# Linear attention feeding a gated MLP: features stationary, plain float32, x divided by token rows, blocks of 512 tokens with 5 and 7 slices

## The chip, the cores and the metric

The kernel runs on one core of a Trainium2 chip. Its time is the device time of one execution in microseconds (us); the median of 3 runs of the kernel before is 1297.62 us (1297.01 to 1298.93).

In the profile the engines are PE (TensorE, matrix multiply), PEld (the weight loads of TensorE, a record for each load), DVE (VectorE), ACT (ScalarE), POOL (GpSimd) and SP (SyncE, which here issues all the DMAs). A matmul has a *stationary* operand, which a weight load puts into the array first, and a *moving* operand, which is streamed past it; "128x65" in a PEld row is a stationary operand of 128 rows and 65 columns, and "128x256" in a PE row is a moving operand of 128 rows and 256 columns.

## The reference

Eight batches, eight heads, 576 tokens, head size D = 64, F = 128 features. `phi` makes 256 features of a token, and the result of the attention is the input x (4608 tokens by 512) of a gated product with 1536 columns:

```python
def phi(x):
    proj = np.einsum('bhsd,df->bhsf', x, w_phi)
    proj = proj - np.max(np.abs(proj), axis=-1, keepdims=True)
    return np.concatenate([np.exp(proj), np.exp(-proj)], axis=-1)
q_p, k_p = phi(q), phi(k)
kv  = np.einsum('bhsf,bhsd->bhfd', k_p, v)
z   = np.sum(k_p, axis=2)
num = np.einsum('bhsf,bhfd->bhsd', q_p, kv)
den = np.einsum('bhsf,bhf->bhs', q_p, z)[..., None] + 1e-06
x   = num / den                        # to (B*S, H*D)
out = ((x @ w_a) * (x @ w_b)) @ w_out
```

All but the three MLP weights is float32. The weights come as float64 and are decoded in the kernel, each into a high and a low float32r part.

## The kernel before

Two number formats are used on TensorE. *Plain* float32 goes in as it is; the trace has two weight loads and two matmul records for each such product. For *float32r* an operand is first split by ACT (a copy, the high part) and DVE (a subtraction, the low part), and a product is then three matmuls, high by high, high by low and low by high, with one record each.

**Attention** works on pairs of heads, 32 in all (8 batches of 4). Of the 576 tokens of a head, 512 are four chunks of 128, and the remaining 64 of two pairs share a "rest" chunk. For a pair:

- `features` projects k: pk (128 tokens by 2 heads by 128 features). The first 9 pairs do it in plain float32; later ones multiply k, stacked as high over low, by `wk2`, which holds the high and low weights side by side (256 moving columns), and ACT and DVE add the two halves. Then DVE takes the maximum and subtracts it, and ACT makes exp(d) and exp(-d).
- `kv_add` accumulates kv transposed: v with a column of ones (65 columns) is stationary, and 256 feature columns move, one matmul for each chunk and head in the first 11 pairs (plain), three in the later ones.
- `k_finish` copies it out, turns it with four transposes and, after pair 7, splits it.
- `q_side` projects q (plain in the first 2 pairs), has POOL take the maximum over partitions, makes the features, splits them and multiplies: kv is stationary (65 columns), 288 tokens move. Numerators go to `xun` and denominators to `den` in DRAM. `reciprocals` makes 1/(den + eps) of a batch by way of DRAM.

**The MLP** runs in two passes over the 12 slices of 128 of the 1536 columns. The first pass, 6 slices in 16 blocks of 288 tokens, fills the time between the attention's instructions and stores its sum in `part`; the second, 6 slices in 9 blocks of 512, comes after the attention and adds `part`. `load_x` loads x and the broadcast reciprocals, multiplies them and splits the product. A block (`moe_block`) then has, for each slice, 12 matmuls into pa and 12 into pb (L515), the product h, its split (L136, L143), and at the end 4 groups of matmuls into po (L538).

**Order.** `attention_steps` gives each piece of a pair a turn number; after each turn up to `PACE` steps of other work (weight decoding, MLP blocks) are emitted. A scheduler then orders the instructions of each engine with a model of their times, and every engine runs its own list in order. Buffers are named by tag with a number of copies; an instruction that writes a new tile waits until the last reader of the old one is done. Of PSUM the MLP has 3 tiles in the attention's time, the attention 4, and kv 1 (in the first batch one of the MLP's).

Of the kernel before, what the change touches and what calls it, by code (L numbers as in the profile page):

```python
# [19 lines left out]
P = 128  # L20
# [3 lines left out]
TURNS0, TURNS, PAIRS0 = 5, 4, 7  # L24
LOAD_TURNS = (-5, -2, -1)
K_TURNS, K_STEP = (0, 3, 5), 2
REST_LOAD_TURNS = (-5, -1, 0)
# [13 lines left out]
ENGINES = {  # L41
    "k_hi": "vss",
    "k_lo": "vvv",
    "v_hi": "sss",
    "v_lo": "vvv",
    "ke_hi": "sss",
    "q_hi": "vss",
    "q_sub": "vvv",
    "qe_hi": "vss",
}  # L50

SLICES0 = 6
T2 = 512
# [3 lines left out]
def tile_kernel(ctx, tc, qT, km, kr, vm, vr, w_phi, w_a, w_b, w_out, out):  # L57
# [20 lines left out]
    X_CHUNKS = 2  # L78
    TS = (HALF, T2)
    NFS = (SLICES0, DF // P - SLICES0)  # L80

# [16 lines left out]

    def products(a, b):

        if len(a) == 1:
            return [(a[0], b[0])]
        return [(a[0], b[0]), (a[0], b[1]), (a[1], b[0])]

    def attention_consts(a1):
# [12 lines left out]
        wk2 = a1.tile([P, 2, F], F32R, name="wk2")  # L118
        nc.vector.memset(wk2.bitcast(F32), 0.0)
        nc.vector.tensor_copy(wk2[:, 0, :], wh)  # L120
        nc.vector.tensor_copy(wk2[:D, 1, :], wl[:D])
        ident = a1.tile([P, P], F32, name="ident")
        make_identity(nc, ident)
        vaug = []
        for i in range(2):
            t = a1.tile([P, NFULL, 2, D + 1], F32R, name=f"vaug{i}")
            nc.vector.memset(t[:, :, :, D : D + 1].bitcast(F32), 1.0)
            vaug.append(t)
        return w2, wh, wl, wk32, wk2, ident, vaug

    def engine(step, b):
        return {"v": nc.vector, "s": nc.scalar}[ENGINES[step][min(b, 2)]]

    def copy(eng, dst, src):
        if eng is nc.scalar:
            eng.copy(dst, src)  # L136
        else:
            eng.tensor_copy(dst, src)

    def split(hi, lo, src, eng_hi, eng_lo):  # L140

        copy(eng_hi, hi, src)
        eng_lo.tensor_tensor(lo, src, hi, op=ALU.subtract)  # L143

    def stack(hi_lo, src, eng_hi, eng_lo):

        copy(eng_hi, hi_lo, src)
        eng_lo.tensor_tensor(hi_lo[D:], src[D:], hi_lo[D:], op=ALU.subtract)  # L148

    def k_load(b, pr, a1, a2, ps, consts, st):  # L150
        vaug = consts[-1]
# [3 lines left out]
        if i < PLAIN_K:  # L155
            k32 = a1.tile([P, n], F32, tag="ks", bufs=2, name=f"k32_{u}")
            nc.sync.dma_start(k32, km[b, pr])
# [4 lines left out]
        if i < PLAIN_KV:  # L162
            v32 = a1.tile([P, NFULL, 2, D + 1], F32, tag="vl", bufs=2, name=f"v32_{u}")
            nc.vector.memset(v32[:, :, :, D : D + 1], 1.0)
        else:
            v32 = a1.tile([P, NFULL, 2, D], F32, tag="v32", name=f"v32_{u}")
        nc.sync.dma_start(v32[:, :, :, :D], vm[b, pr])
        yield
        st["k", b, pr] = (k32,)
        if i >= PLAIN_K:  # L170
            ks = a1.tile([P, 2, n], F32R, tag="ks", bufs=2, name=f"ks_{u}")
# [123 lines left out]
    def spare(b, ps):  # L295

        return (ps_moe, "moe", 3) if b == 0 else (ps, "kvacc", 1)
# [338 lines left out]
```

## Time and profile before

| | |
|---|---|
| median of 3 runs | 1297.62 us |
| the profiled execution, its own time | 1299.35 us |
| its span, first to last instruction | 1297.6 us |
| PE busy | 1253.2 us, 97% |
| PEld busy | 1114.9 us, 86% |
| DVE busy | 841.9 us, 65% |
| ACT busy | 703.1 us, 54% |
| POOL busy | 157.1 us, 12% |
| moved by DMA | 140.12 MB, mean 108 GB/s |

The program has three stages: to about 95 us attention and weight decoding alone, then attention and first pass mixed to 697 us, and after that the rest of the first pass and the second, which run to the end. A busy time of PE is made of records whose ends are modelled, and which overlap; the distance from one record's start to the next is what a matmul costs where PE has no wait.

### The profile page before, as it was taken

The numbers are of one execution on the slowest core, as the hardware profiler recorded it, in microseconds if no ns is written. First come the engines' busy times: TensorE is split into PE (matmuls) and PEld (weight loads), VectorE is DVE, ScalarE is ACT, GpSimd is POOL, SyncE is SP. The second block draws the span as 40 slices with busy tenths as digits, with TensorE's granted clock in tenths as the row PEclk, the third lists the DMA queues.
The fourth block names the chain that finished last, engine by engine and source line by source line (L and its number), as shares of the span: only waits on it lengthen the run. The fifth ranks groups of instructions, "written<-read, shape, count | busy, mean of one in ns | idle before, by whom it ended". The sixth has DMA issues, their size and how long they took to land.

```text
span 1297.6 us, 20263 instructions
## 1 busy us (share of the span) xinstructions
PE 1253.2 (97%) x7632; PEld 1114.9 (86%) x7632; DVE 841.9 (65%) x1388; ACT 703.1 (54%) x1471; POOL 157.1 (12%) x70
## 2 busy tenths in 40 slices
PE   7989879999999999999999999999999999999998
PEld 4558659999999999999999899988888888888887
DVE  5999985798998989988973532698323323333322
ACT  5777775788989888988884322443211211211210
POOL 2323211131222222221220000000000000000000
PEclk9999979999999999999999999999999999999999
DMA  8666532443433435344224821243233133133100
GB/s 197 169 179 177 155 100 77 110 114 107 132 102 112 134 82 156 87 123 123 55 80 117 241 83 56 66 155 110 73 114 98 49 114 98 49 114 96 51 33 33
DMA packets 116594, 140.12 MB, mean 108 GB/s; under 512 B 29136, under 2 KB 81872, under 8 KB 116496
## 3 DMA queue, kind: packets, MB, share of 16 engines
q1 hardware_dynamic: 116496, 138.83, 37.4%
q8 instruction: 60, 0.98, 0.3%
q14 instruction: 38, 0.31, 0.1%
HBM read 110.18 MB, written 28.61 MB: 107 GB/s over the span
## 4 chain that ended last, share of the span: by engine, by line
PE 53%; DVE 7%; ACT 2%; issue 2%; DMA 2%; SPq 0%; DVEq 0%; ACTq 0%
PE po L538 17%; PE pb L515 16%; PE pa L515 16%; PE kvps L286 2%; PE pn L364 2%; DVE qs L148 1%; DVE kel L143 1%; DMA rb<-rec 1%; DVE qel L143 0%; DVE kd L231 0%; DVE kd L234 0%; DVE ks L148 0%; PE pq L340 0%; DMA den<-xn 0%; DVE x L492 0%
## 5 line engine op out<-in xcount | busy, mean ns | idle before, releaser
L344 POOL PARTITION_ALL_REDUCE mb<-p x64 | 156.4, 2444 | 512.8 <-ACT p L341 304.0
L515 PE MATMUL pa<-xh,wh_a 128*128 128x288 f32 (+1 forms) x600 | 200.2, 334 | 5.3 <-DVE h L520 3.1
L538 PE MATMUL po<-hh,wl_o 128*128 128x288 f32 (+1 forms) x600 | 195.8, 331 | 7.2 <-DVE wl_o L433 7.0
L515 PE MATMUL pb<-xh,wh_b 128*128 128x288 f32 (+1 forms) x600 | 198.8, 331 | 4.1 <-ACT h L519 4.1
L520 DVE TENSOR_TENSOR h<-pb,h 128x288 f32<-128x288 f32 (+1 forms) x150 | 80.5, 538 | 185.9 <-PE pb L515 185.2
L515 PE MATMUL pa<-xl,wh_a 128*128 128x288 f32 (+1 forms) x600 | 198.8, 331 | 0.0
L538 PE MATMUL po<-hl,wh_o 128*128 128x288 f32 (+1 forms) x600 | 198.2, 332 | 0.1
L515 PE MATMUL pb<-xl,wh_b 128*128 128x288 f32 (+1 forms) x600 | 198.0, 330 | 0.0
L515 PE MATMUL pa<-xh,wl_a 128*128 128x288 f32 (+1 forms) x600 | 197.8, 330 | 0.0
L515 PE MATMUL pb<-xh,wl_b 128*128 128x288 f32 (+1 forms) x600 | 197.4, 329 | 0.0
L538 PE MATMUL po<-hh,wh_o 128*128 128x288 f32 (+1 forms) x600 | 196.2, 333 | 1.0 <-ACT o L541 0.5
L136 ACT CAST hh<-h 128x288 fp32r<-128x288 f32 (+1 forms) x150 | 75.3, 502 | 192.5 <-DVE h L520 189.8
L519 ACT COPY h<-pa 128x288 f32<-128x288 f32 (+1 forms) x150 | 70.2, 469 | 186.3 <-PE pa L515 184.5
L538 PEld LDWEIGHTS po<-hh,wl_o 128*128 128x128 f32 x600 | 113.2, 189 | 16.6 <-DVE wl_o L433 7.3
L515 PEld LDWEIGHTS pa<-xh,wh_a 128*128 128x128 f32 x600 | 113.3, 189 | 15.8 <-DVE h L520 4.2
L515 PEld LDWEIGHTS pb<-xh,wh_b 128*128 128x128 f32 x600 | 112.9, 188 | 14.7 <-ACT h L519 5.9
L538 PEld LDWEIGHTS po<-hh,wh_o 128*128 128x128 f32 x600 | 112.8, 190 | 11.1 <-DVE h L520 0.9
L538 PEld LDWEIGHTS po<-hl,wh_o 128*128 128x128 f32 x600 | 113.9, 190 | 9.0 <-DVE hl L143 0.4
L515 PEld LDWEIGHTS pa<-xh,wl_a 128*128 128x128 f32 x600 | 113.6, 189 | 8.6
L515 PEld LDWEIGHTS pa<-xl,wh_a 128*128 128x128 f32 x600 | 113.4, 189 | 8.8 <-issue 0.2
L515 PEld LDWEIGHTS pb<-xl,wh_b 128*128 128x128 f32 x600 | 113.0, 188 | 8.5 <-issue 0.2
L515 PEld LDWEIGHTS pb<-xh,wl_b 128*128 128x128 f32 x600 | 112.9, 188 | 8.5
(131 smaller groups left out, 2339.2 us busy)
## 6 DMA issues: line engine op xcount, KB each, us to landing
q<-in_qT SPq DMA_DIRECT2D x124, 144.0 KB
k<-in_km SPq DMA_DIRECT2D x55, 256.0 KB
xun<-xn SPq DMA_DIRECT2D x64, 144.0 KB
x<-xun SPq DMA_DIRECT2D x32, 288.0 KB
rb<-rec SPq DMA_DIRECT2D x64, 144.0 KB
part<-o SPq DMA_DIRECT2D x16, 576.0 KB
o<-part SPq DMA_DIRECT2D x9, 1024.0 KB
v<-in_vm SPq DMA_DIRECT2D x32, 256.0 KB
```

Of the source, the lines that this page charges most:

```text
L136: eng.copy(dst, src)
L143: eng_lo.tensor_tensor(lo, src, hi, op=ALU.subtract)
L148: eng_lo.tensor_tensor(hi_lo[D:], src[D:], hi_lo[D:], op=ALU.subtract)
L286: nc.tensor.matmul(st["kv_ps", b, pr][:width, j], v_[:, j, :width], e_[:, j], start=(left == NFULL and j == 0 and n_ == 0), stop=(left == ...
L344: nc.gpsimd.partition_all_reduce(mb, p32, P, bass_isa.ReduceOp.absmax)
L364: nc.tensor.matmul(pn[: D + 1, :HALF], kv_[:, 2 * j + s, :], e_[:, s, tok], **at)
L515: nc.tensor.matmul(acc, w[:, cc * P : (cc + 1) * P], x, start=(k == 0), stop=(k == 3 * NCC - 1))
L519: nc.scalar.copy(h32, pab["a"])
L520: nc.vector.tensor_tensor(h32, pab["b"], h32, op=ALU.mult)
L538: nc.tensor.matmul(acc, w[:, cc * P : (cc + 1) * P], h, start=(k == 0), stop=(k == 3 * NFS[p] - 1))
```

## The change

- kv is accumulated with the **features stationary** (128 tokens by 128 features) and v with its column of ones moving (65 columns), in plain float32 in all pairs; for each chunk and head two matmuls, one for each sign. The result is already the way round that the numerators want it: no transposes, no split, one ACT copy.
- The **numerators** also have the features stationary (128 features by 128 tokens of q) and kv moving (65 columns), plain float32 in all pairs; a head's 576 tokens are five tiles, the first and the second overlapping by 64. Tokens now lie on partitions, so x is divided at once by its own denominator (`tensor_scalar_add`, `reciprocal`, multiply); `reciprocals`, `den` and `rec` are gone.
- A new step, `x_finish`, turns a pair's x with five transposes on TensorE, splits it into float32r parts, and stores both in DRAM. `load_x` loads the two parts straight into the matmuls' tiles, one copy of each.
- k's float32r projection has 128 moving columns: for each chunk and head two matmuls into the same sum, with the high and with the low weights. `wk2` and the ACT and DVE addition are gone. Plain float32 now in 6 pairs for k and 4 for q.
- Both passes use **blocks of 512 tokens**, the first with 5 slices, the second with 7; the second starts with the two slices whose weights have places of their own. Turns and paces differ a little, and a batch's blocks are queued 2 turns after it is ready.

```diff
-TURNS0, TURNS, PAIRS0 = 5, 4, 7
+TURNS0, TURNS, PAIRS0 = 5, 4, 5
+X_TURN = 13
-DECODE_TURN, BLOCK_LAG = 2, 8
-PACE0, PACE, PACE0_UNTIL = 0.65, 0.9, 18
-PLAIN_K, PLAIN_Q, PLAIN_KV, PLAIN_NUM = 9, 2, 11, 7
-SLICES0 = 6
-T2 = 512
+DECODE_TURN, BLOCK_LAG = 2, 2
+PACE0, PACE, PACE0_UNTIL = 0.65, 0.8, 18
+PLAIN_K, PLAIN_Q = 6, 4
+SLICES0 = 5
+T = 512
...
+    Q_TILES = [slice(0, P)] + [slice(REST + i * P, REST + (i + 1) * P) for i in range(NFULL)]
+    X_CUTS = (0, REST + NFULL // 2 * P, S)
-    xun = [dpool.tile([DM, S], F32, name=f"xun{b}") for b in range(B)]
-    den = [dpool.tile([H, S], F32, name=f"den{b}") for b in range(B)]
-    rec = [dpool.tile([H, S], F32, name=f"rec{b}") for b in range(B)]
+    xparts = [[dpool.tile([DM, S], F32, name=f"x{n}d{b}") for n in "hl"] for b in range(B)]
...
     def features(u, i, k_, c0, n, a2, ps, consts):
-                for j in range(2):
-                    nc.tensor.matmul(pk[:, j], k_[:, j, (c0 + c) * P : (c0 + c + 1) * P], wk2, start=True, stop=True)
-                nc.scalar.copy(kb[:, to], pk[:, :, 1])
-                nc.vector.tensor_tensor(d[:, to], pk[:, :, 0], kb[:, to], op=ALU.add)
+            for j in range(2):
+                nc.tensor.matmul(pk[:, c, j], k_[:, j, tok], wh, start=True, stop=False)
+                nc.tensor.matmul(pk[:, c, j], k_[:, j, tok], wl, start=False, stop=True)
...
-    def kv_add(b, pr, vs, es, st):
-        for j in range(2):
-            parts = products(vs, es)
-            for n_, (v_, e_) in enumerate(parts):
-                nc.tensor.matmul(
-                    st["kv_ps", b, pr][:width, j],
-                    v_[:, j, :width],
-                    e_[:, j],
+    def kv_add(b, pr, v_, e_, st):
+        for j, s in itertools.product(range(2), range(2)):
+            nc.tensor.matmul(
+                st["kv_ps", b, pr][:, j, s, : D + 1],
+                e_[:, j, s],
+                v_[:, j],
...
     def k_finish(b, pr, a1, a2, ps, consts, st):
-        nc.scalar.copy(kvT[: D + 1], st["kv_ps", b, pr][: D + 1].rearrange("p j (s f) -> p (j s) f", s=2))
-        for g in range(4):
-            nc.tensor.transpose(pt[:, g, : D + 1], kvT[: D + 1, g, :], ident[: D + 1, : D + 1])
+        kv = a2.tile([P, 2, 2, D + 1], F32, tag="kv", name=f"kv_{b}_{pr}")
+        nc.scalar.copy(kv, st["kv_ps", b, pr][..., : D + 1])
...
     def q_side(b, pr, j, a1, a2, ps, consts, st):
-            for n_, (s, kv_, e_) in enumerate(parts):
-                at = dict(start=(n_ == 0), stop=(n_ == len(parts) - 1))
-                nc.tensor.matmul(pn[: D + 1, :HALF], kv_[:, 2 * j + s, :], e_[:, s, tok], **at)
-            nc.scalar.copy(xn[: D + 1, tok], pn[: D + 1, :HALF])
-        nc.sync.dma_start(xun[b][h * D : (h + 1) * D], xn[:D])
-        nc.sync.dma_start(den[b][h : h + 1], xn[D : D + 1])
+        pn = ps.tile([P, n, D + 1], F32, tag="att", name=f"pn_{u}")
+        for t, tok in enumerate(Q_TILES):
+            for s in range(2):
+                nc.tensor.matmul(pn[:, t], e[:, s, tok], st["kv", b, pr][:, j, s], start=(s == 0), stop=(s == 1))
+        nc.vector.tensor_scalar_add(r, pn[:, :, D], EPS)
+        nc.vector.reciprocal(r, r)
+        nc.vector.tensor_tensor(x, pn[:, :, :D], r.unsqueeze(2).broadcast_to([P, n, D]), op=ALU.mult)
+
+    def x_finish(b, pr, a1, a2, ps, consts, st):
+        xh, xl = (a2.tile([P, S], F32R, tag=f"x{n}t", bufs=1, name=f"x{n}t_{b}_{pr}") for n in "hl")
+        for lo, hi in zip(X_CUTS, X_CUTS[1:]):
+            pt = ps.tile([P, 512], F32, tag="att", name=f"pt_{b}_{pr}_{lo}")
+            for t, tok in enumerate(Q_TILES):
+                tok = slice(tok.start, REST if t == 0 else tok.stop)
+                if lo <= tok.start < hi:
+                    n = tok.stop - tok.start
+                    nc.tensor.transpose(pt[:, tok.start - lo : tok.stop - lo], x[:n, t], ident[:n, :n])
+            split(xh[:, lo:hi], xl[:, lo:hi], pt[:, : hi - lo])
+        for to, x_ in zip(xparts[b], (xh, xl)):
+            nc.sync.dma_start(to[pr * P : (pr + 1) * P], x_.bitcast(F32))
...
+    def load_x(p, j):
+        xs = [xpool.tile([P, NCC, T], F32R, tag=f"x{n}", name=f"x{n}_{p}_{j}") for n in "hl"]
+            for src, x_ in zip(xparts[b], xs):
+                to = x_[:, :, t - j * T : t - j * T + n]
+                nc.sync.dma_start(to.bitcast(F32), src.rearrange("(c p) s -> p c s", p=P)[:, :, s0 : s0 + n])
...
+    order = [*range(NFS[0], NFS[1]), *range(NFS[0])]
```

More of the change, by code (lines that the diff above doesn't have):

```diff
@@ L117, in attention_consts, with stack, split @@
             nc.vector.tensor_copy(wk32[rows, j, :], w2[rows, :])
[L118 to L121, printed above, removed]
         ident = a1.tile([P, P], F32, name="ident")
         make_identity(nc, ident)
[L124 to L148, printed above, removed]
+        ones = []
+        for name, n, shape in (("va", 3, [P, NFULL, 2, D + 1]), ("rv", 2, [P, 2, D + 1])):
+            ones.append([a1.tile(shape, F32, name=f"{name}{i}") for i in range(n)])
+            for t in ones[-1]:
+                nc.vector.memset(t[..., D : D + 1], 1.0)
+        return w2, wh, wl, wk32, ident, *ones
+    def stack(hi_lo, src):
+        nc.scalar.copy(hi_lo, src)
+        nc.vector.tensor_tensor(hi_lo[D:], src[D:], hi_lo[D:], op=ALU.subtract)
+    def split(hi, lo, src):
+        nc.scalar.copy(hi, src)
+        nc.vector.tensor_tensor(lo, src, hi, op=ALU.subtract)
     def k_load(b, pr, a1, a2, ps, consts, st):
-        vaug = consts[-1]
         u = f"{b}_{pr}"
@@ L242, in features @@
         nc.scalar.activation(e[:, :, 0, :], d, AF.Exp)
         nc.scalar.activation(e[:, :, 1, :], d, AF.Exp, scale=-1.0)
-        es = (e,)
-        if not plain:
-            eh = a2.tile(shape, F32R, tag=f"keh{n}", bufs=n, name=f"keh_{u}")
-            el = a2.tile(shape, F32R, tag=f"kel{n}", bufs=n, name=f"kel_{u}")
-            split(eh, el, e, engine("ke_hi", i // NPAIR), nc.vector)
-            es = (eh, el)
-        yield es
+        yield e
     def k_chunks(b, pr, c0, a1, a2, ps, consts, st):
@@ L534, in moe_block @@
             k = 0
-            for f, (hh, hl) in enumerate(hs):
+            for f, (hh, hl) in hs.items():
                 hi, lo = weights[(p, f, "o")]
@@ L556, in run @@
                 steps -= 1
-    weights, pools_moe, xpools = {}, [ps_moe], [xpool]
-    per = S // TS[0]
+    weights, pools_moe, late = {}, [ps_moe], []
+    blocks = [moe_block(0, j, range(NFS[0])) for j in range(NT // T)]
     with ExitStack() as c:
@@ L589, in tile_kernel @@
     next(last)
-    for f in range(NFS[1]):
+    for f in order:
         if f < NFS[0]:
             next(last)
-        for _ in load_weights(1, f, "ab", wpool if f < NFS[0] else late, stage):
+        for _ in load_weights(1, f, "ab", wpool if f < NFS[0] else late[0], stage):
             pass
     run(deque([last]))
-    first = moe_block(1, 0)
+    first = moe_block(1, 0, order)
     next(first)
-    for f in range(NFS[1]):
+    for f in order:
         next(first)
-        for _ in load_weights(1, f, "o", wpool if f < NFS[0] else late, stage):
+        for _ in load_weights(1, f, "o", wpool if f < NFS[0] else late[0], stage):
             pass
-    run(deque([first] + [moe_block(1, j) for j in range(1, NT // TS[1])]))
+    run(deque([first] + [moe_block(1, j, order) for j in range(1, NT // T)]))
 def kernel(q, k, v, w_phi, moe_w_a, moe_w_b, moe_w_out):
```

255 lines of the change are left out of this document (81 added, 174 removed).

## The prediction

> **What bounds the kernel now.** I read the page first, then busy times by stage, then TensorE's groups kept apart by shape.
>
> ```profile
> span 1297.6 us, 20263 instructions
> PE 1253.2 (97%) x7632; PEld 1114.9 (86%) x7632; DVE 841.9 (65%) x1388; ACT 703.1 (54%) x1471; POOL 157.1 (12%) x70
> ```
>
> By stage (PE, PEld, DVE, ACT, POOL busy; granted clock; DMA):
>
> ```profile
> 0.00:50.00 50.00, 40.15 (x169) 25.55 (x170) 35.71 (x72) 29.49 (x63) 14.61 (x12) 1.00 0.75 188
> 50.00:100.00 50.00, 43.34 (x191) 26.62 (x189) 47.19 (x77) 37.96 (x84) 17.05 (x8) 0.97 0.66 180
> 100.00:150.00 50.00, 48.54 (x297) 39.89 (x296) 47.15 (x85) 37.85 (x83) 10.35 (x4) 1.00 0.59 159
> 150.00:200.00 50.00, 37.34 (x198) 31.76 (x197) 40.90 (x67) 33.73 (x71) 10.43 (x4) 0.83 0.42 118
> 300.00:697.00 397.00, 391.80 (x2990) 381.21 (x2989) 347.15 (x539) 337.44 (x725) 85.56 (x35) 1.00 0.38 103
> 697.00:760.00 63.00, 59.91 (x433) 58.97 (x432) 27.15 (x60) 19.39 (x47) 0.00 (x0) 0.97 0.67 193
> 760.00:1280.00 520.00, 520.00 (x2583) 446.36 (x2582) 212.08 (x358) 129.83 (x236) 0.00 (x0) 1.00 0.26 82
> ```
>
> From 760 us on PE never stops; from 300 to 697 us it stops for 5 us in 397, although DVE and ACT are 85 to 87% busy too. Only in the first 200 us is there idle time to win, 30.6 us of it. So the change is worth what it does to the sum of TensorE's intervals, plus some part of those early waits.
>
> **The price of a matmul now.** Busy times of PE overlap, so I take the distance between starts. The first two rows are pieces of the chain of waits (start, us, what, count), the others the timeline's, where a merged row's count divides the time to the next row.
>
> ```profile
> 757.14 9.58 PE po L538 x72
> 1277.54 16.33 PE po L538 x72
> ```
>
> ```profile
> 22.78 1.89 PE L286 MATMUL kvps<-ke,v 128*65 128x256 f32 x8
> 24.51 1.86 PE L364 MATMUL pn<-qe,kvh 128*65 128x288 f32 x7
> ...
> 321.77 0.28 PE L286 MATMUL kvps<-keh,vaug 128*65 128x256 f32 x1
> ...
> 323.19 0.30 PE L340 MATMUL pq<-qs,wh 128*128 128x288 f32 x1
> ```
>
> A float32r matmul costs 9.58/72 = 133 ns at 288 columns, 16.33/72 = 226.7 at 512, and (323.19 - 321.77)/12 = 118 at 256 (12 kv matmuls stand between). A plain record of 256 columns costs (24.51 - 22.78)/8 = 216, by width 243 at 288; a plain product has two.
>
> Counts, by shape:
>
> ```profile
> L515 PE MATMUL pa<-xh,wh_a 128*128 128x288 f32 x384 | 116.2, 303 | 5.3 <-DVE h L520 3.1 <-ACT xh L136 1.7 <-ACT o L541 0.4
> L515 PE MATMUL pb<-xh,wh_b 128*128 128x512 f32 x216 | 84.1, 389 | 0.0
> L286 PE MATMUL kvps<-keh,vl 128*64 128x256 f32 x168 | 46.9, 279 | 0.0
> L364 PE MATMUL pn<-qel,kvh 128*65 128x288 f32 x200 | 43.8, 301 | 0.2 <-DVE qel L143 0.2
> L286 PE MATMUL kvps<-ke,v 128*65 128x256 f32 x176 | 43.1, 388 | 0.0
> L228 PE MATMUL pk<-wk,ks 128*128 128x256 f32 x184 | 34.3, 286 | 0.0
> L340 PE MATMUL pq<-qs,wl 128*128 128x288 f32 x120 | 34.2, 296 | 0.0
> L364 PE MATMUL pn<-qe,kvh 128*65 128x288 f32 x112 | 31.2, 415 | 5.5 <-DVE kd L234 3.0 <-ACT kvh L311 1.6 <-DVE kd_r L234 0.7
> L219 PE MATMUL pk<-wk,k 128*128 128x256 f32 x72 | 20.5, 412 | 5.3 <-DMA k<-in_km 5.3
> L286 PE MATMUL kvps<-ke_r,rv 64*65 64x256 f32 x48 | 13.1, 390 | 0.0
> L286 PE MATMUL kvps<-keh_r,rvh 64*65 64x256 f32 x40 | 12.1, 303 | 0.0
> ```
>
> Nine MLP forms of 384 and of 216: 3456 x 133 ns + 1944 x 226.7 = 459.6 + 440.7 = 900.3 us. kv: 3 products x (168 + 40 in the rest chunks) x 118 ns + (176 + 48) x 216 = 73.6 + 48.4 = 122.0. Numerators: 600 x 133 ns + 112 x 243 = 107.0. Transposes: 128 x 62 ns (from the weight loads below) = 7.9. k: (184 + 22) x 118 ns + (72 + 10) x 216 = 42.0 (the rest chunks' 22 and 10 are 11 and 5 groups by two). q: 240 x 133 ns (wl as many as wh) + 16 x 243 = 35.8 (2 pairs, 2 heads, 2 halves, 2 records). Attention 314.7, **all 1215.0 us**; the span is 1297.6, so 82.6 us are waits, start and end. The last piece of po ends at 1293.9, 3.7 us before the end, and the first matmul waited 5.3 us for k: 9 us are not to be had.
>
> **The price of the new form.** kv and the numerators now load 128 feature columns for only 65 moving ones. The trace has no such matmul, but it has the load. These are groups of weight loads, then loads and matmuls around one spot where the queue had run dry:
>
> ```profile
> L228 PEld LDWEIGHTS pk<-wk,ks 128*128 128x128 f32 x184 | 28.0, 191 | 0.5 <-ACT p L341 0.2 <-issue 0.2
> L286 PEld LDWEIGHTS kvps<-kel,vaug 128*65 128x65 f32 x168 | 22.8, 135 | 0.0
> L308 PEld LDWEIGHTS pt<-ident,kvT 65*128 65x128 f32 x128 | 12.5, 144 | 3.4 <-ACT kvT L304 1.6 <-issue 1.4
> ```
>
> ```profile
> 22.47 0.33 PEld L308 LDWEIGHTS pt<-ident,kvT 65*128 65x128 f32 x4 [1.37 <-issue]
> ```
>
> ```profile
> 58.27 0.19 PEld L340 LDWEIGHTS pq<-qs,wh 128*128 128x128 f32 x1 [0.39 <-ACT p L341]
> 58.37 0.19 PEld L340 LDWEIGHTS pq<-qs,wl 128*128 128x128 f32 x1
> ...
> 58.27 0.40 PE L340 MATMUL pq<-qs,wh 128*128 128x288 f32 x1
> 58.51 0.29 PE L340 MATMUL pq<-qs,wl 128*128 128x288 f32 x1
> ```
>
> A load of 63 more columns takes 191 - 135 = 56 ns more, 0.89 ns a column: about 110 ns for 128, the rest latency. The spot says the same: the second load starts 0.10 us after the first, and the second matmul 0.24 after it, which is one load (0.107) and one 288-column matmul (0.133) in a row. So a matmul waits for its own load, the next load starts when the array has taken the one before, and a load of 128 columns is hidden today only because a matmul of 256 or 288 columns lasts longer. Transposes load faster: (0.33 - 0.144)/3 = 62 ns for 128 columns. In a plain record 65 columns stream for 216 x 65/256 = 55 ns. So the new record costs its load, 108 ns, and some 6 ns of handing over: **114 ns**, 228 for a product. Bounds: 62 ns (the transposes' pace) and 108 + 55 = 163 (nothing overlaps). I take 114, since the row's shape is that of an ordinary load, and loads do overlap matmuls in every dense row.
>
> k's float32r matmuls of 128 columns load 128 as well: 114 ns each, for a stream that would last about 59. No row has float32r below 256 columns; the bound above is the plain price, 2 x 216 x 128/256 = 216 ns, the bound below again 62.
>
> **The sum after.**
>
> - MLP: (5 x 24 + 4 x 15) x 9 + (7 x 24 + 4 x 21) x 9 = 1620 + 2268 matmuls x 226.7 ns = 881.4 us (19 less: 512 columns carry the fixed part better than 288).
> - kv: 32 pairs x 5 chunks x 4 products x 2 records = 1280 x 114 ns = 145.9 (24 more).
> - Numerators: 64 heads x 5 tiles x 2 signs x 2 records = 1280 x 114 = 145.9 (39 more).
> - Transposes: 160 x 62 = 9.9 (2 more).
> - k: 26 pairs x 4.5 chunks x 4 = 468 x 114 = 53.4, and 27 plain chunks x 2 x 216 = 11.7: 65.1 (23 more).
> - q: 224 x 133 + 32 x 243 = 37.6 (2 more).
>
> All 1285.8 us, **70.8 more than before**.
>
> What is taken from DVE and ACT lies beside PE, so it pays only through the waits:
>
> ```profile
> L143 DVE TENSOR_TENSOR qel<-qe,qeh 128x1152 fp32r<-128x1152 f32 x50 | 68.7, 1374 | 20.5 <-ACT qeh L136 18.4 <-PE pq L340 2.1
> L143 DVE TENSOR_TENSOR kel<-ke,keh 128x1024 fp32r<-128x1024 f32 x42 | 52.8, 1258 | 0.6 <-ACT keh L136 0.4
> L231 DVE TENSOR_TENSOR kd<-pk,kb 128x256 f32<-128x256 f32 x92 | 35.2, 415 | 0.8 <-ACT ke_r L243 0.4
> ```
>
> These three alone are 157 us of DVE, mostly in the attention's time; the new division and `x_finish`'s splits do for each element once what `load_x` does today in both passes, so they add nothing. DVE was 94% busy between 50 and 150 us, and there PE waited; less of that now, and fewer weights to decode early (15 for 18). But in the first pairs (plain today too) DVE loses little. I take 47 us for waits, start and end instead of 82.6; the ends are 25 (9 and a little) and 83 (nothing won).
>
> The x transfers cost nothing as long as they have the po part of a block: 60 or 84 matmuls, 13.6 or 19.0 us, for 2 MB into single tiles, which can start only after the last pb. Today's order, on SP, and the rates there (1.25 us a figure, from 983 us):
>
> ```profile
> 983.83 0.87 SPq L485 DMA_DIRECT2D x<-xun  x2
> ...
> 1001.01 0.59 SPq L548 DMA_DIRECT2D out_x<-o  x1
> ```
>
> ```profile
> GB/s 0 74 340 13 0 10 172 174 358 132 7 0 0 90 202 258 408 293 7 93 380 360 5 0 0 0 0 0 0 0 0 13 0 0 0 0 0 0 0 0
> ```
>
> The load goes out as po begins, ahead of the store; at 340 to 408 GB/s 2 MB take 5 to 6 us.
>
> So 1285.8 + 47 = 1332.8 us of span. The profiled execution lies 1.75 us over its span (1299.35 to 1297.6), and the median 1.73 below the profiled execution: the two cancel, and I forecast a median of **1333 us**, 2.7% slower.
>
> **Rivals.**
>
> 1. *Faster: loads at the transposes' pace.* If plain feature columns load in 62 ns, all 1280 + 1280 + 468 = 3028 records save 52 ns, 157 us: 1176 us. For it: these transposes do load float32 at that pace. Against: theirs last 144 ns, while the ordinary 128-column loads last 191. The point of decision: 36 us over 3028 records, 12 ns; a record must cost under 102 ns for the kernel not to be slower. The Trainium skill ("TensorE: Matmul & The Clock Gate", Back-to-back issue gap) gives about 81 ns a matmul for a sustained stream of loads and matmuls at N = 128; by it the three forms would be 100 us cheaper than at 114, some 1233 us. The same sentence gives 131 ns for N = 512, where this trace has 226.7, so I hold little of it for 4-byte operands.
> 2. *Narrow float32r at the plain price.* k's 468 matmuls at 216 instead of 114 ns: 48 us more, 1381 us. For it: the kernel before went out of its way to make 256 columns, by `wk2`. Against: no row shows a dependence on width but the streaming itself.
> 3. *x comes late.* If SP puts the load behind the store, or the one copy of x is freed late, each of 17 blocks waits some 6 us: 102 us, 1435. Against: the order above.
> 4. *The early waits vanish altogether* and loads need no handing over: 3028 x 6 = 18 us and 20 us of waits less, 1295: no change.
>
> **Chances.** Forecast 0.66 (own range 1302 to 1369, the two ends of the waits, loads at 108 to 114); rival 1 0.14; rival 2 0.13; rival 3 0.03; rival 4 0.04. The range 1300 to 1390 holds the forecast and rival 2 and leaves out 1 and 3. A measurement of this kernel tells about 0.2% from no change; faster by more 0.14, within 0.04, slower 0.82.
>
> **What would show it.** In the timeline a kv chunk pair of 16 records should take 1.8 us (rival 1: 1.0) with the next record's load starting as each matmul starts; the numerators' 20 records 2.3 us; four narrow k matmuls 0.46 us (rival 2: 0.86). pa's twelve matmuls should stay at 2.72 us in the last stage, which should be 514 us long, 73 longer than 1944 matmuls are now, while the stages before it lose little or nothing. Idle PE between 0 and 200 us should fall below 30 us. I am wrong if TensorE's intervals sum to less than 1250 us, or if waits take more than 83.

## The result, and the profile after

The changed kernel takes 1388.78 us (median of 4 runs, 1378.36 to 1395.91) where the kernel before takes 1298.28 beside it: a ratio of 1.0687 (95% interval 1.0603 to 1.0772). It is 6.9% slower; the forecast was 2.7%. The direction was right, and the size was missed by 56 us. The spread is new as well: the kernel before stays within 5 us, the changed one moves by 17, and by 26 with the four runs of a later repetition (experiment 4). A ratio here leaves out runs that took over 1.5% longer than the fastest of their kernel, which changes a figure in one place: the second run of experiment 6, where the ratio rests on two of its four times and the median on all.

The page of the changed kernel, its totals and the granted clock in 40 equal slices of the span, in tenths:

```profile
span 1376.6 us, 18489 instructions
PE 1347.7 (98%) x7386; PEld 1162.8 (84%) x7386; DVE 616.6 (45%) x1053; ACT 493.5 (36%) x932; POOL 142.8 (10%) x70
...
PEclk9678999999998999999999999999999999999999
```

DVE and ACT are much relieved (45 and 36% busy, from 65 and 54), and PE is 98% busy. Over the whole span PE is idle for 28.9 us (1376.6 - 1347.7), where the kernel before had 44.4 (1297.6 - 1253.2). Taken alone, that reads like a denser TensorE kernel. But the second to fourth slices of PEclk say 6, 7 and 8.

The changed kernel by stage (from and to, length, then PE, PEld, DVE, ACT and POOL busy with counts, granted clock, DMA share, GB/s):

```profile
0.00:50.00 50.00, 41.52 (x222) 34.14 (x223) 34.30 (x70) 24.48 (x49) 12.17 (x11) 0.88 0.66 168
50.00:100.00 50.00, 47.55 (x246) 42.52 (x246) 47.30 (x83) 28.90 (x58) 11.96 (x5) 0.70 0.57 163
100.00:150.00 50.00, 44.91 (x259) 38.98 (x258) 33.46 (x60) 25.06 (x51) 6.92 (x3) 0.87 0.50 140
150.00:200.00 50.00, 50.00 (x325) 44.97 (x325) 24.61 (x42) 23.92 (x46) 8.56 (x4) 1.00 0.39 109
...
770.00:860.00 90.00, 84.59 (x367) 70.00 (x368) 58.64 (x108) 34.34 (x59) 0.00 (x0) 0.96 0.55 184
```

Idle PE in the first 200 us is 16.0 us (8.5 + 2.4 + 5.1 + 0), where it was 30.6 before; 5.3 of the 16.0 are the start's wait for k, as before, and 4.9 are new waits for x. Between 770 and 860 us, where the two passes meet, it is 5.4 us. Yet from 50 to 100 us the clock was 0.70 on average, so for some 30 of these 50 us PE ran at half its clock, and that time counts as busy. The clock in smaller stretches:

```profile
37.00:61.00 24.00, 21.49 (x79) 18.33 (x80) 20.68 (x40) 13.38 (x27) 4.56 (x2) 0.51 0.40 127
61.00:82.00 21.00, 18.69 (x130) 16.19 (x128) 20.25 (x37) 12.97 (x26) 5.13 (x2) 0.99 0.73 208
82.00:103.00 21.00, 20.86 (x89) 18.79 (x87) 19.34 (x34) 11.34 (x24) 4.51 (x2) 0.51 0.55 154
```

There are only two values, half and full. At half clock PE does some 80 to 90 records in 21 to 24 us and looks as busy as at full clock, where it does 130 in 21 us.

The prices, from the changed kernel's timeline (start, us, engine, line, matmul, shapes, count); the distance to the next row divided by the count is the price of one record. The first two rows lie in a stretch of half clock, the others at full clock:

```profile
41.69 4.53 PE L268 MATMUL pn<-kv,qe 128*128 128x65 f32 x20
46.01 2.02 PE L169 MATMUL pk<-wk,k 128*128 128x256 f32 x4
...
297.85 2.34 PE L268 MATMUL pn<-kv,qe 128*128 128x65 f32 x20
300.00 0.31 PE L172 MATMUL pk<-wh,ks 128*128 128x128 f32 x1
300.93 2.62 PE L216 MATMUL kvps<-va,ke 128*128 128x65 f32 x22
303.47 0.86 PE L289 MATMUL pt<-ident,x 64*128 64x64 f32 x5
304.17 2.34 PE L268 MATMUL pn<-kv,qe 128*128 128x65 f32 x20
```

At full clock: numerators (300.00 - 297.85)/20 = 108 ns, eight narrow float32r matmuls (300.93 - 300.00)/8 = 116, kv (303.47 - 300.93)/22 = 115, transposes (304.17 - 303.47)/5 = 140. At half clock a numerator record takes (46.01 - 41.69)/20 = 216 ns: the load doubles like the rest.

With the medians of such distances over the whole trace, the intervals sum to kv 139.5, numerators 139.1, transposes 20.3, k 68.4, q 39.5 and MLP 881.2: 1288.2 us, where 1285.8 was forecast. The span is 1376.6, so 88.4 us are waits, start, end and slow stretches, where 47 were forecast. Such a sum is known to about 1%: with medians over single records, instead of rows of the timeline, it is 1295.6 us (1221.0 for the kernel before), which leaves 81.0 us beside it (76.6 before).

The waits of PE before and after, in two fences (line, what for, us in total, times, longest). The kernel before:

```profile
PE po L538 <- DVE wl_o L433: 7.0, 2, 4.8
...
PE pq L340 <- DVE qs L148: 4.2, 4, 2.2
PE pb L515 <- ACT h L519: 4.1, 6, 1.1
PE pa L515 <- DVE h L520: 3.1, 4, 1.8
PE pn L364 <- DVE kd L234: 3.0, 2, 1.7
```

The changed kernel:

```profile
PE pa L413 <- issue: 7.1, 1, 7.1
...
PE pa L413 <- DMA xh<-xhd: 4.8, 4, 3.3
PE pq L252 <- DVE kd L178: 2.6, 2, 2.3
PE pq L252 <- issue: 2.5, 1, 2.5
PE pa L413 <- DMA xl<-xld: 1.9, 2, 1.6
```

Before, the list is led by DVE and ACT, which have 34 us in the whole of it. After, they are left with 3.3 us, 2.6 of them in the row above, and the first matmul of an MLP block waits for x instead: 4.8 and 1.9 us by name. The 7.1 us "issue" are x too, by the timeline of all engines there:

```profile
767.42 0.86 PE L289 MATMUL pt<-ident,x 64*128 64x64 f32 x5
768.10 0.70 ACT L116 CAST xht<-pt 128x320 fp32r<-128x320 f32 x2
768.83 0.32 SPq L292 DMA_DIRECT2D xhd<-xht  x1
769.41 0.97 SPq L292 DMA_DIRECT2D xld<-xlt  x1
773.07 0.37 SPq L394 DMA_DIRECT2D xh<-xhd  x1
...
775.41 0.76 PE L413 MATMUL pa<-xh,wh_a 128*128 128x512 f32 x1 [7.13 <-issue]
```

The last pair's x is turned, split, stored to DRAM, loaded back and then multiplied; SP issues the load 3.7 us after the store, and PE starts 7.1 us after its last transpose's end.

In summary, the sum of intervals came out nearly as forecast. Two things that the forecast did not contain stand where the old waits were: a clock that is halved for some 55 of the first 140 us, and x that comes late. The runs now separate them.

### The profile page after: what moved, and what is told of

Read it like the earlier page. It is cut to its first block, busy times and chain, and to the rows that moved or that the text cites. A ratio compares the mean times of both kernels' runs of the same rounds, so it can differ in the third digit from the quotient of the medians.

```text
span 1376.6 us, 18489 instructions
## 1 busy us (share of the span) xinstructions
PE 1347.7 (98%) x7386; PEld 1162.8 (84%) x7386; DVE 616.6 (45%) x1053; ACT 493.5 (36%) x932; POOL 142.8 (10%) x70
## 4 chain that ended last, share of the span: by engine, by line
PE 91%; DMA 4%; DVE 3%; issue 1%; ACT 1%; POOL 0%; SPq 0%; ACTq 0%
PE pa L413 22%; PE po L437 22%; PE pb L413 21%; PE pn L268 9%; PE kvps L216 9%; PE pq L252 3%; PE pt L289 2%; PE pk L173 2%; PE pk L172 1%; DMA xl<-xld 1%; DMA xh<-xhd 1%; PE pk L169 1%; DMA xld<-xlt 1%; DMA xhd<-xht 0%; DVE p L257 0%
## 5 line engine op out<-in xcount | busy, mean ns | idle before, releaser
L413 PE MATMUL pa<-xh,wh_a 128*128 128x512 f32 x432 | 172.4, 399 | 11.9 <-issue 7.1
L413 PE MATMUL pa<-xl,wh_a 128*128 128x512 f32 x432 | 171.0, 396 | 1.9 <-DMA xl<-xld 1.9
L413 PE MATMUL pa<-xh,wl_a 128*128 128x512 f32 x432 | 170.0, 394 | 0.0
L437 PE MATMUL po<-hh,wh_o 128*128 128x512 f32 x432 | 169.7, 394 | 0.0
L413 PE MATMUL pb<-xh,wh_b 128*128 128x512 f32 x432 | 169.0, 391 | 0.0
L437 PE MATMUL po<-hl,wh_o 128*128 128x512 f32 x432 | 168.8, 391 | 0.0
L437 PE MATMUL po<-hh,wl_o 128*128 128x512 f32 x432 | 168.6, 390 | 0.0
L413 PE MATMUL pb<-xh,wl_b 128*128 128x512 f32 x432 | 168.3, 390 | 0.0
L413 PE MATMUL pb<-xl,wh_b 128*128 128x512 f32 x432 | 168.2, 389 | 0.0
L268 PE MATMUL pn<-kv,qe 128*128 128x65 f32 x1280 | 161.5, 284 | 0.2
L413 PEld LDWEIGHTS pa<-xh,wh_a 128*128 128x128 f32 x432 | 82.6, 191 | 29.3 <-issue 7.8
```

The source lines that it names most:

```text
L268: nc.tensor.matmul(pn[:, t], e[:, s, tok], st["kv", b, pr][:, j, s], start=(s == 0), stop=(s == 1))
L413: nc.tensor.matmul(acc, w, x[:, cc], start=(k == 0), stop=(k == 3 * NCC - 1))
L437: nc.tensor.matmul(acc, w[:, cc * P : (cc + 1) * P], h, start=(k == 0), stop=(k == 3 * NFS[p] - 1))
```

## The experiments

In what follows, *halved time* is twice the missing share of the granted clock times the span: 77 us in the profiled run of the changed kernel, (1 - 0.972) x 2 x 1376.6, and 23 to 29 in most runs of the kernel before. All edits are to the changed kernel, unless "before" is said.

**1. Wider moving operands.** If a record costs its load, moving columns are free up to about 128. In kv 128 columns of v now move, in the numerators 102; the products that nobody needs are computed and not read.

```diff
-                st["kv_ps", b, pr][:, j, s, : D + 1],
+                st["kv_ps", b, pr][:, j, s],
                 e_[:, j, s],
-                v_[:, j],
+                v_.rearrange("p j d -> p (j d)")[:, 2 * j : 2 * j + P],
...
-        kv = a2.tile([P, 2, 2, D + 1], F32, ...)
-        nc.scalar.copy(kv, st["kv_ps", b, pr][..., : D + 1])
+        kv = a2.tile([P, 2, 2, P], F32, ...)
+        nc.scalar.copy(kv, st["kv_ps", b, pr])
...
+        wide = 512 // n
+        at, to = (0, 0) if j == 0 else (P - wide, wide - D - 1)
-                nc.tensor.matmul(pn[:, t], e[:, s, tok], st["kv", b, pr][:, j, s], ...)
+                nc.tensor.matmul(pn[:, t], e[:, s, tok], st["kv", b, pr][:, j, s, at : at + wide], ...)
```

> The changed kernel with the same weight loads and the same count of records, but wider moving operands in the two new forms: kv moves 128 columns instead of 65 (63 of them the other head's, not used), the numerators 102 instead of 65. Three theories. Load: a record costs the load of its 128 stationary columns, so both forms stay at 112 ns although the array streams 2.0 and 1.6 times as much; were streaming the price, kv would go to some 213 ns and the kernel would be over 130 us slower. Clock: the changed kernel had its TensorE clock halved for 77 us of its profiled run (23.9, 20.5, 10.2, 13.7 and 6.8 us at a time, where the kernel before had 3.4 at a time), because the array streams only 55 of 112 ns; with the wider stream the halved time falls below 25 us in all and the kernel is 25 to 45 us faster than the changed one's 1388.8, between 1345 and 1365. Waits: the clock only follows the waits of the schedule, the width has no part in it, and the time stays between 1378 and 1396.

Measured: 1356.88 us (1355.34 to 1359.09), ratio 1.0444 (1.042 to 1.0467). A kernel that streams more columns in every attention matmul is 32 us faster. The timeline of this kernel, read as above:

```profile
280.02 2.37 PE L270 MATMUL pn<-kv,qe 128*128 128x102 f32 x20
282.17 0.31 PE L172 MATMUL pk<-wh,ks 128*128 128x128 f32 x1
...
283.10 2.67 PE L216 MATMUL kvps<-va,ke 128*128 128x128 f32 x22
285.70 0.86 PE L291 MATMUL pt<-ident,x 64*128 64x64 f32 x5
```

A numerator record takes 2.15/20 = 108 ns, as with 65 columns, and a kv record 2.60/22 = 118, 3 ns more. So a record's price doesn't follow its stream, as the forecast had it, and the gain comes from elsewhere. The clock of the same stretches says where:

```profile
37.00:61.00 24.00, 21.07 (x126) 17.83 (x127) 21.59 (x41) 14.95 (x32) 5.43 (x3) 0.86 0.48 145
82.00:103.00 21.00, 20.22 (x158) 18.72 (x158) 20.19 (x36) 17.45 (x35) 7.07 (x3) 1.00 0.80 236
```

The clock is 0.86 and 1.00 instead of 0.51, and PE does 126 and 158 records where it did 79 and 89. Halved time is 16 to 24 us in the four runs, and the spread of their times has shrunk to 4 us.

**2. Half a load.** In kv only 64 of the 128 features are loaded. This leaves out the other half of the features; their place in kv takes a copy of the first half's sums.

```diff
-                st["kv_ps", b, pr][:, j, s, : D + 1],
-                e_[:, j, s],
+                st["kv_ps", b, pr][:REST, j, s, : D + 1],
+                e_[:, j, s, :REST],
...
```

> The changed kernel with 64 instead of 128 stationary columns in kv's 1280 records: half of the features are left out of kv (the second half of the features takes the first half's sums), all else is kept. Load: a record of kv falls from 112 ns to about 61 (55 for the load, 6 for handing over), 65 us less in all, near 1320. Were the price a fixed one for each record or the streaming of 65 columns in four passes, kv's records would stay at 112 ns and the time near 1389. Clock: with the array streaming 55 of 61 ns in kv, less of the halved time, so it may be 70 to 85 us less.

Measured: 1335.99 us (1332.35 to 1338.91), ratio 1.0276 (1.0249 to 1.0303). The groups and the timeline show kv at about half its price. Within a row of the timeline the next record mostly starts 55 to 61 ns later:

```profile
L216 PEld LDWEIGHTS kvps<-va,ke 128*64 128x64 f32 x1024 | 70.0, 145 | 18.1 <-issue 13.6 <-ACT ke L182 0.7 <-ACT wh_a L348 0.7
```

```profile
297.70 1.15 PE L216 MATMUL kvps<-va,ke 128*64 128x65 f32 x16
```

So a record is bound by its load, seen from both sides: halve the load and the price goes from 109 (139.5 us by 1280) to 60 ns, double the stream and it hardly moves. 1280 records save 49 ns each, 63 us; 53 were measured between the medians. Part of the difference is in the waits: PE is idle for 35.1 us here, 6 more than in the changed kernel. The rest was not followed up. Halved time stays at 61 to 83 us: the numerators, in which the first slow stretch begins, are as narrow as ever.

**3. The numerators alone wide**, kv as changed. To fill the wider tile, `k_finish` now makes four ACT copies instead of one.

```diff
-        kv = a2.tile([P, 2, 2, D + 1], F32, ...)
+        kv = a2.tile([P, 2, 2, P], F32, ...)
...
-                nc.tensor.matmul(pn[:, t], e[:, s, tok], st["kv", b, pr][:, j, s], ...)
+                nc.tensor.matmul(pn[:, t], e[:, s, tok], st["kv", b, pr][:, j, s, at : at + wide], ...)
```

> The changed kernel with the numerators alone moving 102 columns instead of 65 (the array streams 85 of their 112 ns), kv as in the changed kernel (55 of 112). Clock: halved time between the wide kernel's 17 us and the changed kernel's 77 to 128, so 1362 to 1378, and less spread between runs than 1378 to 1396. Waits: no change from the changed kernel.

Measured: 1372.20 us (1370.38 to 1373.08), ratio 1.0553 (1.053 to 1.0577), with 60 to 69 us of halved time. Half of the cure gives about half of the effect: 1388.8, 1372.2 and 1356.9 us with none, one and both of the forms widened, and none of these ranges overlaps another. That speaks for the streaming as the cause, and against an accident of timing that any edit would have removed.

**4. The changed kernel again**, for the relation between clock and time.

> The changed kernel itself once more, so that it stands on the same chip as the combinations below: 1378 to 1396, with the halved clock between 77 and 130 us of each run and the time going with it, some 0.3 to 0.5 us for each us of halved clock.

Measured: 1395.14 us (1374.89 to 1400.98), a little beyond the expected range at both ends. With the first four runs, eight pairs of time and halved time (us):

```
1374.89/60  1378.36/77  1382.73/86  1393.48/114
1394.84/123 1395.91/128 1396.80/126 1400.98/146
```

They lie along a line of about 0.3 us of time for 1 us of halved time ((1400.98 - 1374.89)/(146 - 60)). So the kernel's spread is the clock's. A straight line through the eight pairs is 1354.8 us and 0.325 us for each us of halved time, and all eight lie within 2 us of it. At the 16 us of experiment 1 it gives 1360, where 1356.9 was measured: the clock accounts for nearly all of that gain. The profile of this execution, by the clock:

```profile
39.00:91.00 52.00, 51.73 (x195) 44.27 (x195) 36.37 (x68) 22.50 (x44) 9.05 (x4) 0.51 0.41 121
101.00:142.00 41.00, 37.43 (x162) 35.55 (x163) 31.52 (x56) 20.23 (x40) 6.64 (x3) 0.50 0.60 172
```

In the first of these PE is 51.73 us busy in 52, and the clock does not come back. The drop comes right after a wait of 2.5 us (which the changed kernel's list has too, as "pq L252 <- issue"), but what follows is dense, and the clock stays at half for 51 us.

**5. Blocks queued later.** The changed kernel queues a batch's blocks 2 turns after x is ready, the kernel before 8.

```diff
-DECODE_TURN, BLOCK_LAG = 2, 2
+DECODE_TURN, BLOCK_LAG = 2, 8
```

> The changed kernel with a batch's blocks queued 8 turns after it is ready, as before, instead of 2. Waits: the first block's waits for x (3.6 and 2.0 us near 115 us) vanish, 1370 to 1385. Clock: the early stretch with narrow streams alone gets longer, nothing mixes into it, and the halved time with it: 1389 or above.

Measured: 1361.79 us (1358.95 to 1367.90), ratio 1.0478 (1.0435 to 1.0521): 27 us better, more than either theory gave it. Its waits of PE:

```profile
PE pk L169 <- DMA k<-in_km: 5.1, 1, 5.1
PE pt L289 <- ACT qe L261: 4.5, 1, 4.5
```

None for x is left. Halved time is 54 to 74 us, also less than the changed kernel's, so this edit touches both causes: the order of the early work changes with it. At its median of 64 us the line of experiment 4 gives 1375.6, 13 us of the gain; the other 14 us are what the waits for x came to in the changed kernel (4.8, 1.9 and 7.1). To part the two by a run, the same edit was made on top of experiment 1, where the clock is full nearly all the time.

> The changed kernel with the wide moving operands of kv and the numerators and with the queueing 8 turns after a batch is ready. Each alone took 27 to 32 us off. If they remove different things (the halved clock; the waits for x at the blocks' starts, 15 to 20 us of gaps), both together give 1335 to 1345; if the later queueing worked through the clock, no more than the wide kernel alone, 1352 to 1360.

Measured: 1343.58 us (1342.54 to 1346.81), ratio 1.0342 (1.0323 to 1.0361), halved time 8 to 16 us. On the wide kernel, 8 turns are worth 13.3 us (1356.88 - 1343.58). Its waits for x come to 4.1 us, where the wide kernel with 2 turns has 12.0 (7.1 of "issue", 3.7 and 1.2). First the wide kernel with 2 turns, then with 8:

```profile
PE pa L415 <- issue: 7.1, 1, 7.1
...
PE pa L415 <- DMA xl<-xld: 3.7, 1, 3.7
```

```profile
PE pa L415 <- DMA xl<-xld: 2.2, 1, 2.2
PE pa L415 <- DMA xh<-xhd: 1.9, 1, 1.9
```

So 8 of the 13 us are waits for x by name; some 3 are halved time (16 to 24 us down to 8 to 16), and the rest goes with the other order. The two edits take 32 and 27 us alone and 45 together, so they overlap, as they must if the later queue acts on the clock too. Is an early queue bad for any kernel?

```diff
 (before)
-DECODE_TURN, BLOCK_LAG = 2, 8
+DECODE_TURN, BLOCK_LAG = 2, 2
```

> The kernel before with a batch's blocks queued 2 turns after it is ready instead of 8. If early queueing brings waits for x by itself, as in the changed kernel, 1305 to 1320; if the waits there come from x in one copy of each part, no change, 1296 to 1302.

Measured: 1299.84 us (1295.11 to 1301.91), ratio 1.0002 (0.9989 to 1.0016). In the kernel before it makes no difference. What makes the changed kernel sensitive (x through DRAM as two finished parts, one copy of each tile, nothing of `load_x` on DVE in between) was argued from the timeline above; no run isolates it.

**6. k's projection.** First the narrow form alone, in the kernel before, with the ACT and DVE addition gone:

```diff
 (before)
-                    nc.tensor.matmul(pk[:, j], k_[:, j, (c0 + c) * P : (c0 + c + 1) * P], wk2, start=True, stop=True)
...
-                nc.scalar.copy(kb[:, to], pk[:, :, 1])
-                nc.vector.tensor_tensor(d[:, to], pk[:, :, 0], kb[:, to], op=ALU.add)
+                    nc.tensor.matmul(pk[:, c, j], k_[:, j, tok], wh, start=True, stop=False)
+                    nc.tensor.matmul(pk[:, c, j], k_[:, j, tok], wl, start=False, stop=True)
```

> The kernel before with one part of the change, k's float32r projection with 128 moving columns, twice as many matmuls, and without the ACT copy and DVE addition. Load: 206 records at 118 ns become 412 at 112, 22 us more on TensorE; DVE loses 40 us of work off the path, so 10 to 22 us more, 1308 to 1320. If narrow float32r went at the plain price (216 ns) it would be 65 us more, 1363. If the waits for DVE were what bound the attention's time, it would be no slower or faster than 1298.

Measured: 1311.79 us (1310.91 to 1313.29), ratio 1.0092 (1.0073 to 1.0112). The price from its timeline, six matmuls from the first row to the second:

```profile
301.70 0.28 PE L229 MATMUL pk<-wl,ks 128*128 128x128 f32 x1
...
302.37 0.27 PE L229 MATMUL pk<-wl,ks 128*128 128x128 f32 x1
```

0.67/6 = 112 ns, the load again, so rival 2 (216) is out. By the prediction's counts 206 matmuls of 118 ns become 412 of 112, 22 us more; 12 were measured. The relief of ACT and DVE may pay the rest back; PE's idle time did fall by 6 us (44.4 to 38.1). Then the reverse, `wk2` put back into the changed kernel:

```diff
...
-                nc.tensor.matmul(pk[:, c, j], k_[:, j, tok], wh, start=True, stop=False)
-                nc.tensor.matmul(pk[:, c, j], k_[:, j, tok], wl, start=False, stop=True)
+                    nc.tensor.matmul(pk[:, j], k_[:, j, (c0 + c) * P : (c0 + c + 1) * P], wk2, start=True, stop=True)
...
+                nc.scalar.copy(kb[:, to], pk[:, :, 1])
+                nc.vector.tensor_tensor(d[:, to], pk[:, :, 0], kb[:, to], op=ALU.add)
```

> The changed kernel with that one part undone: k's float32r projection moves high and low weights side by side (256 columns), ACT copies and DVE adds. Load: 468 records at 112 ns become 234 at 118, 25 us less on TensorE, 1355 to 1370, since DVE was only 45% busy. Waits: the added DVE and ACT work brings the waits back, and the time stays at 1380 or above.

Measured: 1367.48 us (1355.43 to 1379.41), ratio 1.044 (1.0408 to 1.0473), 21 us better, and still with 68 to 132 us of halved time and the spread that belongs to it. At equal halved time its four runs lie 18 to 21 us under the line of experiment 4, so the gain is not the clock's. And with experiments 1 and 5 together, so that the clock is full:

> The changed kernel with the wider moving operands in kv and the numerators (the clock stays up) and with k's float32r projection 256 columns wide again. If the two causes are separate and add, it is 25 us below the wide kernel's 1356.9, 1328 to 1336; if the added ACT and DVE work of the projection brings waits, 1340 or above.

Measured: 1342.84 us (1341.61 to 1345.17), ratio 1.0332 (1.0307 to 1.0356), 14 us under experiment 1, of the 25 that the count of records gives: the second expectation, waits, holds for the other part. PE is idle for 35.6 us, 8.3 more than in experiment 1: its waits for x by name grow from 4.9 to 8.5, and those on ACT and DVE from 3 to 8. With blocks queued 8 turns after x is ready as well:

> The same with k's float32r projection 256 columns wide again: what is left of the change are kv and the numerators with 128-column loads and the MLP's blocks. The sum of TensorE's intervals is about 1264 us, so with 50 to 60 us of waits 1314 to 1326: still slower than the kernel before, by about what the loads of kv and the numerators cost more (49 and the transposes' 13) less the blocks' 19 us and some waits.

Measured: 1322.52 us (1321.00 to 1322.74), ratio 1.0174 (1.0158 to 1.0189). This is the changed kernel with the clock, the early queue and k's narrow projection all mended, and it is still 1.7% slower than the kernel before. What is left in it of the change's cost is the loads of kv and the numerators (65 more moving columns would be free there), against which stands the gain of the larger blocks; this split is by the sum, not by a run.

**7. The blocks alone**, in the kernel before: a first pass of 5 slices in 12 blocks of 384 tokens (512 do not fit beside the other tiles), the second of 7. To make room, several staging tiles have one copy fewer.

```diff
 (before)
-SLICES0 = 6
+SLICES0 = 5
+T1 = 384
-    X_CHUNKS = 2
-    TS = (HALF, T2)
+    X_CHUNKS = 1
+    TS = (T1, T2)
...
```

> The kernel before, attention untouched, with the change's idea for the MLP as far as memory allows: first pass in 12 blocks of 384 tokens and 5 slices, second in 9 of 512 and 7 (x loaded one chunk at a time, fewer staging buffers in the last stage). By the sum of intervals: 12 x 180 x 173 ns (between 133 at 288 and 226.7 at 512 columns) + 2268 x 226.7 = 888 us for 900, 12 us less, 1280 to 1294. If the second pass's weight decoding with fewer buffers becomes the bound, it is 1300 or more.

Measured: 1338.26 us (1335.78 to 1340.94), ratio 1.0295 (1.0266 to 1.0323). This was a miss: 1280 to 1294 were expected. The sum of intervals did fall, by 10 to 13 us as one counts, but the span of its profile is 1338.4, 40.8 longer, so the time beside the sum rose by some 52. PE's idle time makes 34 of it (44.4 to 78.3), and its list of waits is led by x's two parts, 21.6 us, where the kernel before waited 1.7:

```profile
PE pa L516 <- ACT xh L137: 11.1, 8, 3.8
PE pa L516 <- DVE xl L144: 10.5, 10, 2.6
```

In its stage beside the attention:

```profile
300.00:697.00 397.00, 372.50 (x2418) 354.34 (x2417) 337.95 (x492) 326.65 (x670) 84.20 (x35) 0.98 0.39 108
```

PE is busy for 372.5 us, where the kernel before had 391.8 in the same stretch. DVE and ACT, at 82 to 85%, deliver a larger block's x too late. Loading x one chunk at a time and the fewer staging copies may have a share in that, and the clock has one (45 to 53 us of halved time, where the kernel before has 23 to 29); the run doesn't part them. It suggests, without showing it, that larger blocks need the idle DVE and ACT that the rest of the change makes.

**8. The other way to fill the array**, in the kernel before. If the load of a short stationary operand hides behind 256 moving columns, then 128 stationary columns cost no more than 65. In the 21 later pairs, kv's stationary operand is v's high part, the column of ones and v's low part side by side: two matmuls for each chunk and head instead of three; `k_finish` adds the halves after the transposes. One column of v's low part does not fit and is left out.

```diff
 (before)
-            vl = a1.tile([P, NFULL, 2, D + 1], F32R, tag="vl", ...)
-            split(va[:, :, :, :D], vl[:, :, :, :D], v32, ...)
-            st["v", b, pr] = (va, vl)
+            copy(engine("v_hi", b), va[:, :, :, :D], v32)
+            nc.vector.tensor_tensor(va[:, :, :, D + 1 :], v32[:, :, :, : D - 1], va[:, :, :, : D - 1], op=ALU.subtract)
+            st["v", b, pr] = (va,)
...
-            parts = products(vs, es)
+            parts = [(vs[0], e_) for e_ in es]
...
+            src = a2.tile([P, 4, D + 1], F32, tag="kvs", ...)
+            nc.scalar.copy(src, pt[:, :, : D + 1])
+            nc.vector.tensor_tensor(src[:, :, : D - 1], pt[:, :, D + 1 :], src[:, :, : D - 1], op=ALU.add)
```

> The kernel before, with kv's stationary operand in the 21 later pairs filled up from 65 to 128 columns: v's high part, the column of ones and the low part of 63 of the 64 columns side by side, so two matmuls with 256 moving columns for each chunk and head instead of three (the low part of one column of v is left out; k_finish adds the two halves after the transposes, one ACT copy and one DVE addition more for a pair). Load as the larger of load and stream: a load of 128 columns (112 ns) is hidden behind 256 columns (118 ns), so 624 records become 416 at the same 118 ns, 24.5 us less; the transposes' wider moving operand gives 4 back (84 at 109 for 62 ns): about 20 us less, 1276 to 1284, and faster than both kernels. If a longer load has a price of its own beside the stream, the records go to 160 ns or more and the time stays at 1295 or above.

Measured: 1283.57 us (1278.51 to 1285.29, 5 runs), ratio 0.9869 (0.9847 to 0.989): faster than both kernels. Its timeline, seven matmuls from the first row to the second:

```profile
324.84 0.28 PE L283 MATMUL kvps<-kel,vs 128*65 128x256 f32 x1
...
325.67 0.28 PE L283 MATMUL kvps<-keh,vs 128*128 128x256 f32 x1
```

0.83/7 = 119 ns, over rows that alternate between 128 and 65 stationary columns. About 208 matmuls at 118 ns, 25 us, are gone; 15 to 17 of them are left in the time (by the medians, 1298.88 - 1283.57, or by the ratio), after the additions in `k_finish`.

## Why the prediction was right in direction and wrong in size

**The price of the new form, "114 ns": right.** Measured 108 to 116 at full clock, for plain records and for narrow float32r alike, and experiments 1 and 2 show from both sides that it is the load. Rival 1 (62 ns) and rival 2 (216 ns) are out. That the measured 1388.8 us lies near rival 2's 1381, and inside the prediction's wider range of 1300 to 1390, is chance: k's matmuls kept the forecast's price, and what made up the difference was something else. The 81 ns that the Trainium skill ("TensorE: Matmul & The Clock Gate", Back-to-back issue gap) gives for 128 columns is not reached by these forms either.

**The sum, 1285.8 us: right in total,** 1288.2 measured, or 1295.6 by single records. By rows of the timeline two terms were off and cancel: kv and numerators together 13 us less than forecast (109 ns a record on average), the transposes 10 us more. Of the transposes I had taken the load's price, 62 ns; these move 128 columns where the old ones moved 65, and take 109 ns, and 203 where one of 64 rows is followed by another form. k was 3 us dearer, q 2.

**The last stage: right.** The second pass ran from 858.5 to 1372.7 us, 514 us, as forecast. Idle PE in the first 200 us was 16 us, under the 30 named. In that rival 4 was half right: half of the early waits did go. But I had named idle time as the sign, and a halved clock is busy time: the sign came out as forecast while the stage was losing.

**"I take 47 us for waits, start and end instead of 82.6": this step failed.** 88.4 us were found, more than the 83 that the prediction had named as its sign of being wrong, and that in the fastest of the four runs. Of its two halves, one held: DVE and ACT were relieved, and the waits on them shrank (of the rows shown, from 21 us to 2.6; of all, from 34 to 3.3). The other did not: that nothing new would stand in their place, and that a busy PE runs at its full clock. What the runs put there, against the forecast of 1333:

- the halved clock, 32 us (1388.8 to 1356.9, by experiment 1; 28 by the line of experiment 4)
- blocks that are queued before their x is there, 13 us (1356.9 to 1343.6, by experiment 5 on the wide kernel; 8 of them named as waits for x)
- the remaining 11 us: with both edits the sum by single records is 1294.2 us and the time beside it 47.4, so the sum is 73 us above the kernel before, where 71 were forecast, and the time beside it 29 below, where 36 were forecast. What is left over is 2 us of the sum, 6 of waits that did not shrink as far as hoped, and 2 between the span and the median.

The forecast's 47 us is thus about what this kernel has once its clock and its queue are mended. One end of the prediction's own range doesn't follow from its terms: with loads at 108 ns and 25 us of waits it is 1293 us, not 1302. The result lies beyond the other end.

**"The x transfers cost nothing", "against: the order above" (rival 3): wrong in part.** Not each of 17 blocks waits 6 us: six waits for x make 6.7 us together, the longest 3.3, and the block whose x is made last waits 7.1. I had looked at the steady second pass, where the load does go ahead of the store and comes in time, and not at the blocks that are queued 2 turns behind the pair that makes their x. `BLOCK_LAG` was in the diff, as "a batch's blocks are queued 2 turns after it is ready", and I gave it no price.

**The halved clock could have been asked of the trace before.** There the clock is 0.83 between 150 and 200 us, a row that the prediction itself shows, right where PE was idle for 12.7 us. I read the row for its idle time alone. What could not be read is that the new records, streaming for an estimated 55 of their 109 ns, would keep the clock down once it had dropped.

## What to carry to other kernels

In these runs an ordinary matmul cost about the longer of its load and its stream, so count what the array does in that time: 128 stationary columns behind 256 moving ones are free (and bought 1.3% here), while 65 moving columns behind a load of 128 leave half of the record empty. Read the granted clock beside every busy share, since a TensorE that is 98% busy may be busy at half speed; where only a short stream can follow a load, widening it with columns that nobody needs can be worth more than it costs. And where the distance between a producer and the work that reads it through DRAM is cut, price the last one of the chain, not the steady state.

## What the runs showed of the hardware that was not expected

- **A sparse stream keeps the clock down.** In the kernel before, the clock drops to half after waits of TensorE of 1.6 to 4.8 us, and in the two profiled executions of the changed one of 1.7 to 7.1 us, or, at 406 us, of only 0.7. In the kernel before it is back after 3.4 us, in one case 6.8; in the changed one it stays down for 10 to 51 us with PE 85 to 100% busy (6.8 us in one place, at the late block at 771 us), and with both forms wide it is back after 3.4 to 6.8. Here is one drop of the kernel before, 10 us with a clock of 0.83, which is 3.4 us at half, and the changed kernel's stretch from 406 us, in which PE never pauses:

```profile
90.00:100.00 10.00, 7.15 (x28) 4.17 (x27) 8.10 (x16) 6.59 (x15) 2.79 (x2) 0.83 0.81 189
```

```profile
406.30:420.00 13.70, 13.70 (x57) 12.87 (x56) 6.17 (x12) 4.91 (x10) 2.74 (x1) 0.50 0.55 128
```

The Trainium skill ("TensorE: Matmul & The Clock Gate", Part 1: the HAM clock gate) says that the gate follows how busy the engine has recently been, and that about 3.4 us of sustained work bring the full clock back. By that rule the 52 us stretch of experiment 4, 51.73 of them busy, should have recovered at once, and did not; the rule fits these runs only if "busy" means streaming, not occupied. How large a share of streaming it takes is not known from these runs. A new record streams for 55 of 109 ns (by the prediction's figure for 65 columns), and a wide one, by the same scale, for 86 of 108 or 108 of 118. But the new records fill only some 14 us each of the changed kernel's first two stretches of 24 and 20 us, and wider matmuls of k and q the rest, so the clock stays down at more than a half.
- **The load slows with the clock** as the stream does: 216 ns a record at half clock, 108 at full.
- **Float32r with 128 moving columns** costs its load and little more, 112 to 116 ns; at 128 columns, half of the 256 that the kernel before keeps to, a matmul did not get dearer.
- **One halved microsecond costs 0.3 us** here, by the eight pairs of experiment 4, not the 0.5 that half the work undone would make. Part of the slow time may cover waits that PE would have had anyway; that was not shown.
